# Low parts of the first tile's second half of keys, and of the gate sums, moved behind the second head's minimum in a planned attention and MLP kernel

## The chip, the cores and the metric

The kernel runs on one NeuronCore of a Trainium2 chip. The metric is device time in microseconds of one execution, as a median over timed runs. The core has five instruction queues that matter here: TensorE (PE in the profile, with its weight loads as PEld), VectorE (DVE), ScalarE (ACT), GpSimd (POOL) and SyncE (SP), which issues the DMA transfers.

## What is computed

Attention with a forget gate over 4 batches of 8 heads, 576 positions, head size 64, all in float32; then two MLPs, each over 2304 rows of 512:

```python
log_f = np.log(np.clip(f, 0.0001, 1.0))
cum = np.cumsum(log_f, axis=-1)
scores = q @ k.T / sqrt(64) + (cum[..., :, None] - cum[..., None, :])
attn = softmax(where(causal, -1e9, scores))
x = attn @ v                                  # heads side by side: 2304 x 512
h = x @ w_in                                  # d_ff 1024
solu = h * softmax(h)
x = (layernorm(solu) * g_ln) @ w_out
out = relu(x @ w2_in) ** 2 @ w2_out           # d_ff 2048
```

## The kernel before

**Split operands.** A float32 value is kept as a rounded high part and a low part, the difference, and a product is made of three products of parts. So each operand needs a copy or cast for its high part and a subtraction for its low part. For the scores, the two halves of TensorE's 128 rows carry the parts: `K1` holds high parts of the keys twice, `K2` holds the low parts in its first 64 rows and, below them, 16 rows with the parts of the gate sums (`cum`) of all heads; `Q2` has rows of zeros and ones there, its picks, that take the head's own row. `KN` and `QN` are the raw keys and queries as loaded. The index `j` is the half of the heads: `j = 0` for heads 0 to 3, `j = 1` for heads 4 to 7.

**Tiles and stages.** A tile is 128 (or, once a batch, 64) query positions of one batch, for all 8 heads; there are 20. `head(s)` puts down one head of one tile: the scores in a PSUM bank `z` (line 576, two matmuls a cut), the minimum over the masked row on VectorE (`least`, line 597), the exponential on ScalarE (line 611), transposes of the result by TensorE (line 630) and copies of them back to SBUF (line 376 on ScalarE, 382 on VectorE). `mix` multiplies with the values (line 650). Two banks `z` alternate between the heads, three buffers hold exponentials, three banks `pp` transposes. Where 128 rows of x are done, `first(x)` puts down the first MLP for them: matmuls (lines 869 to 871), a softmax and norm with two long ScalarE operations (887, 908), transposes of the result, and `out1` with the second half (lines 820 to 822). Between all this, the weights of the MLPs are split: line 729 and 378 on ScalarE, 733 and 737 on VectorE, 743 and 747 on GpSimd or VectorE. After about 450 us the second MLP runs.

**What sets the order.** Nothing is issued as it is written. `pl.add` makes a `Step` with a cost on each engine that may do it, a priority (a due time), and the keys that it reads and writes, from which its dependences follow. `Plan.lay` then walks a clock of its own: at each point it takes, on each engine, the ready step that can start first, and among those that can start within `slack` the one with the lowest priority. A step with several engines goes to the one that is free first. Steps marked `port=True` on VectorE and steps of GpSimd are laid one after the other in this clock. So a step that is moved changes what is ready when, and with it the choice of engine and the order of everything that follows.

In this clock, where TensorE would stand idle for over 400 ns in the first 140 us, `fill` puts in filler transposes (line 1706) that compute nothing, as many as fill 0.6 of the hole at 62 ns each.

**What the change touches.** At the start stand priorities of their own:

```python
SECOND, THIRD = 9900.0, 9000.0
```

`SECOND` is the due time of what the first tile's heads 4 to 7 need: the copies of keys and queries and their low parts (`prep_k`, low parts in line 498; `prep_q`, scalings in lines 378 to 384, low parts in line 541). `THIRD` is that of the gate sums beyond the first tile: the scan over 448 positions (named line 1575 in the profile), their high part (a copy on ScalarE, line 1606) and their low part (line 1609, `tensor_tensor` of 32 x 576). Both parts are written to DRAM (`cumd`, line 1554) and come back, spread over the heads, as the 16 rows of `K2` for each later tile (line 506). The first tile's heads start at due time 10000, later than both.

Of the kernel before, what the change touches and what calls it, by code (L numbers as in the profile page):

```python
# [27 lines left out]
class Plan:  # L28
# [11 lines left out]
        dve=dict(pe=230, dve=127, act=198, pool=203, dma=1230),  # L40
# [19 lines left out]
    def add(self, eng, fn, prio, reads=(), writes=(), take=None, uses=(), late=0, port=False, kind="r"):  # L60

        s = Step()
        s.eng, s.fn, s.prio, s.take, s.no, s.late = eng, fn, prio, take, len(self.steps), late
        deps = {}
        s.uses = tuple(uses) + ((take,) if take else ())
        for k in s.uses:  # L70
            self.users.setdefault(k, []).append(s)
        s.weak, s.port, s.kind = None, port, kind
        for k in reads:
            if k in self.writer:
                deps[self.writer[k].no] = self.writer[k]
            rs = self.readers.setdefault(k, [])
            if k in self.banks or k[0] in ("pp", "hp"):

                if rs and rs[-1].no not in deps:
                    s.weak = rs[-1]  # L80
                    deps[s.weak.no] = s.weak
            rs.append(s)
        for k in writes:
            if k in self.writer:
                deps[self.writer[k].no] = self.writer[k]
            for r in self.readers.get(k, ()):
                deps[r.no] = r
        for k in writes:
            self.writer[k] = s
            self.readers[k] = []  # L90
        deps.pop(s.no, None)
        s.deps = list(deps.values())
        s.succ = []
        for d in s.deps:
            d.succ.append(s)
        s.left = len(s.deps)
        s.rdy = {}
        s.end = None
        self.steps.append(s)
        return s  # L100

    def fill(self, order, ring, a, b, lag, share):
        ident = self.writer["ident"]
# [165 lines left out]
def tile_kernel(ctx: ExitStack, tc: tile.TileContext, q, k, v, f, w_in, w_out, g_ln, w2_in, w2_out, out):  # L269
# [23 lines left out]
    HH = H // 2  # L293
# [66 lines left out]
    pl = Plan(dict(pp=3, hp=2, rq=NRQ), ("z0", "z1", "xo", "h", "h0", "h1"))  # L360
# [83 lines left out]


    vslot = {}

    def load_k(n, prio):
        T = tiles[n]
# [36 lines left out]
    def prep_k(n, prio):  # L486
        T = tiles[n]
        m, b, q0 = T["m"], T["b"], T["q0"]
        kc = kcol(b, T["t"])
        cs = slice(kc, kc + m)  # L490
        los = {}
        for j in range(2):
# [15 lines left out]
            if n == 0 and j:  # L508
                prio = SECOND
# [6 lines left out]
                lo, prio + 2 * j, [("kn", j)] + hk, lk,  # L516
                port=True,
            )
            for y in range(2):
                rk = [f"cumd{y}"] if n else [("c0", 0), ("xh", 0, 0)][y : y + 1]  # L520
                pl.add(
                    dict(dma=350), lambda y=y, auxrows=auxrows: auxrows(y), (prio if n else -7e6) + 2 * j, rk,
                    writes=kcells(f"ka{y}", j, kc, kc + m),
                )

    def prep_q(n, prio):
        m = tiles[n]["m"]
        i = n % 2
        raw = QN[:, 0 : HH * m].rearrange("p (h s) -> p h s", s=m)
        for j, src in enumerate(own):  # L530
# [9 lines left out]
            def lo(src=src, q1=q1, hi=(q1 if j else q2)):  # L540
# [2 lines left out]
                    op1=ALU.subtract,  # L543
                )

            pl.add(
                dict(dve=67 + 1.045 * HH * m), lo, prio + 2 * j, ["qn", ("qd" if j else "qh", i, j)], [("ql", i, j)],
                port=True,
            )


    def head(s):
# [48 lines left out]

        for y, (c, k_) in enumerate(zip(cuts, zk)):
            w = c[2] - c[1]
            pl.add(
                dict(dve=77 + 1.042 * w + 61 * y), lambda y=y, c=c: least(y, c), prio,
                ["mask"] + [sk_ + (0,)] * y, [k_, sk_ + (y,)],
            )
# [962 lines left out]
    for y, (a, e) in enumerate(((0, P), (P, S))):  # L1570
# [33 lines left out]
        ["mhalf", ("lf", 0), ("lf", 1), ("qh", 0, 0), ("qd", 0, 0)], [("st", 0, 0)],  # L1604
    )
    pl.add(dict(act=573), lambda: nc.scalar.copy(part(0), cu), THIRD, ["cu0", "cu1"], pt0[0])
    pl.add(
        dict(dve=669),
        lambda: nc.vector.tensor_tensor(out=part(1), in0=cu, in1=part(0).bitcast(F32), op=ALU.subtract), THIRD,
        ["cu0", "cu1"] + pt0[0], pt0[1],  # L1610
# [38 lines left out]
    for n in range(NQ):  # L1649
        for h in range(H):  # L1650
# [7 lines left out]
            if h == PQ and n + 1 < NQ:  # L1658
                prep_q(n + 1, when[s])
                if n + 2 < NQ:  # L1660
                    load_q(n + 2, when[s])
            head(s)
            w = 4 if n >= QUADS else 2
            if (h + 1) % w == 0:
                mix(s, w)
# [129 lines left out]
```

## Time and profile before

| | us |
|---|---|
| median of 3 timed runs (lowest, highest) | 810.95 (810.48, 811.85) |
| the profiled execution, its own time | 813.03 |
| the profiled execution, its span | 811.2 |
| TensorE busy in the span | 790.8 (97%) |
| VectorE busy | 638.9 (79%) |
| ScalarE busy | 550.3 (68%) |
| GpSimd busy | 384.6 (47%) |

The span is what the hardware profiler saw between the first and the last instruction; the execution's own time has what lies around it as well. Busy times are sums over the span, and a share over the whole span mixes stages with different limits: the attention stage, up to some 450 us, keeps four engines going, while in the MLP stage behind it TensorE alone is at its limit. Fillers count as busy time of TensorE. The granted TensorE clock is 1.00 of full speed in every stretch up to 780 us.

### The profile page before, as it was taken

The page shows a single profiled execution, that of the slowest core. Times are in us where ns is not written, and L with a number is a line of the kernel's source. Part 1 is how long each engine was busy: PE and PEld are TensorE (multiplying, and loading weights), DVE is VectorE, ACT ScalarE, POOL GpSimd, SP SyncE. Part 2 cuts the span into 40 slices and gives each one's busy share as a digit, 9 for nine tenths or more (in the row PEclk, how much of TensorE's full clock was granted, in tenths as well). Part 3 has the DMA queues.
Part 4 walks back from the last instruction along what each step waited for, and adds up shares of the span by engine and source line. Part 5 has one row for each costly group of instructions (what it writes and reads, how often), then busy time and mean ns, then how long its engine had stood idle before and what let it go on. Part 6 is the DMA issues. An engine that isn't in the chain of part 4 may idle for free.

```text
span 811.2 us, 19134 instructions
## 1 busy us (share of the span) xinstructions
PE 790.8 (97%) x6607; PEld 726.7 (90%) x6607; DVE 638.9 (79%) x1627; ACT 550.3 (68%) x1425; POOL 384.6 (47%) x520
## 2 busy tenths in 40 slices
PE   7899999999999999999999999999999999999997
PEld 6677788888888888888989999999999999999997
DVE  8788788787786667886677879779778877987777
ACT  6899998889998888898886775445335343533442
POOL 6467778666778686777757622120211121112110
PEclk9999999999999999999999999999999999999999
DMA  6644346656664555665477899696767767675401
GB/s 216 206 117 140 105 128 186 206 173 190 199 206 163 189 171 165 196 229 180 169 247 232 265 309 368 213 321 212 229 207 233 230 203 223 216 232 186 159 1 53
DMA packets 109665, 159.69 MB, mean 197 GB/s; under 512 B 12832, under 2 KB 52768, under 8 KB 109568
## 3 DMA queue, kind: packets, MB, share of 16 engines
q1 hardware_dynamic: 109280, 158.21, 60.9%
q8 instruction: 52, 0.85, 0.4%
q14 instruction: 45, 0.37, 0.2%
q10 hardware_dynamic: 288, 0.26, 0.1%
HBM read 121.65 MB, written 36.72 MB: 195 GB/s over the span
## 4 chain that ended last, share of the span: by engine, by line
PE 47%; POOL 2%; DVE 2%; issue 1%; DMA 1%; ACT 1%; DVEq 0%; POOLq 0%
PE z L1392 9%; PE pp L1392 9%; PE hp L1497 4%; PE hp L1498 4%; PE hp L1499 4%; PE z L1341 3%; PE xo L1498 2%; PE xo L1499 2%; PE xo L1497 2%; DMA w2d<-free 1%; PE pp L1498 1%; PE pp L1499 1%; PE pp L1497 1%; PE pp L820 1%; PE pp L822 1%
## 5 line engine op out<-in xcount | busy, mean ns | idle before, releaser
L611 ACT ACTIVATE adj<-z,st 64x288 f32<-64x288 f32 (+9 forms) x192 | 95.0, 498 | 17.7 <-DVE st L597 15.9
L576 PE MATMUL z<-k,q 80*64 80x288 f32 (+17 forms) x384 | 89.9, 331 | 0.2
L597 DVE CUSTOM_DVE_ANT_0 z<-z,maskb 128x128 f32<-128x128 f32 (+8 forms) x144 | 65.3, 462 | 26.8 <-PE z L576 24.8
L630 PE MATMUL pp<-ident,adj 128*128 128x128 f32 (+1 forms) x480 | 76.4, 273 | 9.2 <-ACT adj L611 8.2
L821 PE MATMUL pp<-ln,wol 128*128 128x256 f32 x288 | 80.1, 278 | 0.0
L822 PE MATMUL pp<-ln,woh 128*128 128x256 f32 x288 | 80.1, 278 | 0.0
L630 PEld LDWEIGHTS pp<-ident,adj 128*128 128x128 f32 (+1 forms) x480 | 50.7, 140 | 32.4 <-ACT adj L611 22.4
L376 ACT COPY pt<-pp 128x384 f32<-128x384 f32 (+5 forms) x167 | 67.5, 422 | 15.2 <-PE pp L630 13.7
L1153 DVE TENSOR_TENSOR k<-adj,k 128x512 fp32r<-128x512 f32 (+1 forms) x71 | 48.9, 688 | 32.5 <-POOL k L380 25.2
L743 POOL TENSOR_TENSOR free<-free 128x256 uint32<-128x256 uint32 x64 | 49.1, 772 | 33.9 <-DVE free L737 20.7
L576 PEld LDWEIGHTS z<-k,q 128*128 128x128 f32 (+3 forms) x384 | 54.9, 176 | 8.3 <-ACT adj L611 4.1
L869 PE MATMUL hp<-wih,xl 128*128 128x512 f32 x144 | 60.0, 417 | 0.8 <-ACT hp L908 0.8
L650 PE MATMUL xo<-pt,vn 128*64 128x128 f32 (+1 forms) x960 | 60.4, 268 | 0.1
L650 PEld LDWEIGHTS xo<-pt,vn 128*64 128x64 f32 x960 | 48.6, 137 | 9.4 <-issue 5.4
L870 PE MATMUL hp<-wil,xh 128*128 128x512 f32 x144 | 56.6, 393 | 0.2 <-DVE wil L747 0.2
L871 PE MATMUL hp<-wih,xh 128*128 128x512 f32 x144 | 56.8, 394 | 0.0
L1106 POOL TENSOR_TENSOR free<-free 128x256 f32<-128x256 f32 x64 | 52.5, 821 | 7.5 <-DMA w2d<-free 4.8
L821 PEld LDWEIGHTS pp<-ln,wol 128*128 128x128 f32 x288 | 54.4, 189 | 0.4
L822 PEld LDWEIGHTS pp<-ln,woh 128*128 128x128 f32 x288 | 54.1, 188 | 0.0
L1098 POOL TENSOR_TENSOR free<-free 128x256 fp32r<-128x256 f32 x63 | 50.0, 805 | 7.4 <-ACT free L376 6.9
L380 POOL TENSOR_SCALAR k<-adj 128x512 fp32r<-128x512 f32 x37 | 23.1, 624 | 63.7 <-PE xo L1499 25.7
L1392 PE MATMUL z<-wol,k 128*128 128x256 f32 x384 | 52.4, 276 | 0.0
(614 smaller groups left out, 2682.4 us busy)
## 6 DMA issues: line engine op xcount, KB each, us to landing
k<-w2u SPq DMA_DIRECT2D x96, 256.0 KB
ln<-w2u SPq DMA_DIRECT2D x96, 256.0 KB
w2u<-free SPq DMA_DIRECT2D x56, 256.0 KB
kn<-in_k_dram SPq DMA_DIRECT2D x32, 256.0 KB
free<-in_moe_w_out_dram SPq DMA_DIRECT2D x32, 256.0 KB
free<-in_moe_w_in_dram SPq DMA_DIRECT2D x32, 256.0 KB
q<-w2u SPq DMA_DIRECT2D x32, 256.0 KB
w2f<-free SPq DMA_DIRECT2D x49, 128.0 KB
```

What stands on the lines that cost most here:

```text
L376: nc.scalar.copy(dst(), src())
L576: nc.tensor.matmul(dst, lhsT=ql[0:r, p, 0:m], rhs=rhs, start=(g == 0), stop=(g == 1))
L597: nc.vector.tensor_tensor_reduce(out=z, in0=z, in1=maskb[0:m, o : o + e - a], scale=1.0, scalar=st[0:m, 0:1] if y else 3e38, op0=ALU.add, ...
L611: nc.scalar.activation(out=adj[0:m, c[1] : c[2]], in_=Z[c[0]][0:m, 0 : c[2] - c[1]], func=AF.Exp, bias=st[0:m, low : low + 1], scale=-1.0, ...
L630: nc.tensor.transpose(at(sk)[:, (c - g) * m : (c - g + 1) * m], adj[0:m, zc : zc + P], ident[0:m, 0:m])
L650: nc.tensor.matmul(XO[own[j], g // 2, off : off + m], lhsT=VN[vslot[b, c]][:, (g + j) * D : (g + j + 1) * D], rhs=PT[(s - h + g + j) % NPT ...
L821: nc.tensor.matmul(px, lhsT=wol[:, fc, w], rhs=hi, start=False, stop=False)
L822: nc.tensor.matmul(px, lhsT=woh[:, fc, w], rhs=hi, start=False, stop=(fc == KF - 1))
L869: nc.tensor.matmul(HP[:, c], lhsT=XL[i][:, cc, :], rhs=wih[:, cc, w], start=(cc == 0), stop=False)
L871: nc.tensor.matmul(HP[:, c], lhsT=XH[i][:, cc, :], rhs=wih[:, cc, w], start=False, stop=(cc == KC - 1))
L1392: nc.tensor.matmul(half(i), lhsT=l, rhs=r[:, c * TB : c * TB + TB], start=(j == start), stop=(j == 5), skip_group_check=True,)
L1497: nc.tensor.matmul(po, lhsT=gl, rhs=wh, start=(p == 0 and i in opens), stop=False, skip_group_check=True)
```

## The change

It adds two dependences between steps of the plan and moves one priority by 2: no operation of the computation is added or removed. Two low parts may not start before the minimum of the first tile's head 1: that of the first tile's keys of heads 4 to 7, and that of the gate sums. (`least_of[1, 0]` is the step of that minimum; `held_back` gets one step, since only the first tile's `j = 1` is put in.) The low part of the first tile's queries of heads 4 to 7 gets the priority `SECOND` instead of `SECOND + 2`.

```diff
+    def after(self, s, d):
+        if d not in s.deps:
+            s.deps.append(d)
+            d.succ.append(s)
+            s.left += 1
...
+    held_back, least_of = [], {}
...
+            if n == 0 and j:
+                held_back.append(los[j])
...
-            pl.add(
-                dict(dve=67 + 1.045 * HH * m), lo, prio + 2 * j, ["qn", ("qd" if j else "qh", i, j)], [("ql", i, j)],
-                port=True,
+            s = pl.add(
+                dict(dve=67 + 1.045 * HH * m), lo, SECOND if n == 0 and j else prio + 2 * j,
+                ["qn", ("qd" if j else "qh", i, j)], [("ql", i, j)], port=True,
             )
...
-            pl.add(
+            least_of[s, y] = pl.add(
                 dict(dve=77 + 1.042 * w + 61 * y), lambda y=y, c=c: least(y, c), prio,
...
-    pl.add(
+    low_sums = pl.add(
         dict(dve=669),
...
             head(s)
+            if s == 1:
+                for x in held_back + [low_sums]:
+                    pl.after(x, least_of[1, 0])
```

The lines of the new file are 6 to 12 higher: 597 becomes 606, 498 becomes 505, 384 becomes 390, 541 becomes 550, 1609 becomes 1618, 482 becomes 489, 743 becomes 752, 747 becomes 756, 820 becomes 829, 576 becomes 585, 630 becomes 639, 947 becomes 956 and 1706 becomes 1718. What the plan makes of it is shown at three places.

VectorE, first tile, behind the scan of the gate sums. `k_8` is `K2` of heads 4 to 7, `q_20` is `Q2`, `q_42` is `Q1` of heads 4 to 7, `free` the gate sums, and the two rows that write `z` and `st` are minima (each with a row that reads the result out). Before:

```order
L498 TENSOR_TENSOR k_8_79<-kn_17_88,k_46_117 64x4x128
L384 TENSOR_SCALAR q_20_91<-qn_80 64x512
L1609 TENSOR_TENSOR free_92<-free_92 32x576
L597 ISA z_121,st_29_100<-z_121,maskb_71 128x128
L597 ISA st_29_100 128x1
L597 ISA z_122,st_30_101<-z_122,maskb_71 128x128
L597 ISA st_30_101 128x1
L384 TENSOR_SCALAR q_42_113<-qn_80 64x512
L541 SCALAR_TENSOR_TENSOR q_42_113<-qn_80,q_42_113 64x512
L597 ISA z_121,st_31_102<-z_121,maskb_71 128x128
```

Now:

```order
L390 TENSOR_SCALAR q_20_91<-qn_80 64x512
L390 TENSOR_SCALAR q_42_113<-qn_80 64x512
L550 SCALAR_TENSOR_TENSOR q_42_113<-qn_80,q_42_113 64x512
L606 ISA z_121,st_29_100<-z_121,maskb_71 128x128
L606 ISA st_29_100 128x1
L606 ISA z_122,st_30_101<-z_122,maskb_71 128x128
L606 ISA st_30_101 128x1
L1618 TENSOR_TENSOR free_92<-free_92 32x576
L505 TENSOR_TENSOR k_8_79<-kn_17_88,k_46_117 64x4x128
L606 ISA z_121,st_31_102<-z_121,maskb_71 128x128
```

The low part of the keys and that of the gate sums stood ahead of the first two minima and now stand behind them; the second scaling of the queries and their low part (now lines 390 and 550) stood behind and are now ahead.

GpSimd, from its picks (`q_20<-ident`) on. `k_7` and `k_8` in lines 498 and 505 are here the low parts of the second tile's keys, `ln` and `wil` parts of the first MLP's weights. Before:

```order
L482 TENSOR_TENSOR q_20_91<-ident_110 16x512
L380 TENSOR_SCALAR ln_50_209<-ln_50_209 128x512
L498 TENSOR_TENSOR k_7_78<-kn_16_87,k_45_116 64x4x128
L498 TENSOR_TENSOR k_8_79<-kn_17_88,k_46_117 64x4x128
L743 TENSOR_TENSOR ln_50_209<-ln_50_209 128x512
L380 TENSOR_SCALAR ln_50_209<-ln_50_209 128x512
L743 TENSOR_TENSOR ln_50_209<-ln_50_209 128x512
```

Now:

```order
L489 TENSOR_TENSOR q_20_91<-ident_110 16x512
L386 TENSOR_SCALAR ln_50_209<-ln_50_209 128x512
L752 TENSOR_TENSOR ln_50_209<-ln_50_209 128x512
L756 TENSOR_TENSOR wil_75<-ln_50_209,wih_74 128x512
L386 TENSOR_SCALAR q_20_91<-qn_80 64x512
L386 TENSOR_SCALAR ln_50_209<-ln_50_209 128x512
L752 TENSOR_TENSOR ln_50_209<-ln_50_209 128x512
```

The two low parts of the second tile's keys have left this queue. They are in VectorE's now: one ahead of the minimum of head 4 (the picks of line 489, which stood ahead of it, now behind it), one ahead of the minimum of head 7.

TensorE, in the first tile of 64 rows (the fifth tile), where each head has two cuts of 288 columns, up to the first matmuls of `out1`. Line 947 (now 956) transposes the normalised rows that `out1` needs. Before:

```order
L947 MATMUL pp_125<-ident_110,e_90 128x128 x4
L947 MATMUL pp_126<-ident_110,e_90 128x128 x4
L869 MATMUL hp<-wih_74,xl_38_109 128x512
L870 MATMUL hp<-wil_75,xh_37_108 128x512
L871 MATMUL hp<-wih_74,xh_37_108 128x512
L576 MATMUL z_121<-k_45_116,q_41_112 64x288
L576 MATMUL z_121<-k_7_78,q_20_91 64x288
L576 MATMUL z_122<-k_45_116,q_41_112 64x288
L576 MATMUL z_122<-k_7_78,q_20_91 64x288
L630 MATMUL pp_127<-ident_110,adj_28_99 128x64 x5
L820 MATMUL pp_125<-ln1a_857,woh_76 128x256
```

Now:

```order
L585 MATMUL z_122<-k_45_116,q_41_112 64x288
L585 MATMUL z_122<-k_7_78,q_20_91 64x288
L639 MATMUL pp_127<-ident_110,adj_27_98 128x64 x5
L1718 MATMUL pp_126<-ident_110 128x128 x18
L956 MATMUL pp_126<-ident_110,e_90 128x128 x4
L956 MATMUL pp_125<-ident_110,e_90 128x128 x4
L585 MATMUL z_121<-k_46_117,q_42_113 64x288
L585 MATMUL z_121<-k_8_79,q_20_91 64x288
L1718 MATMUL pp_127<-ident_110 128x128 x10
L585 MATMUL z_122<-k_46_117,q_42_113 64x288
L585 MATMUL z_122<-k_8_79,q_20_91 64x288
L829 MATMUL pp_127<-ln1a_817,woh_76 128x256
```

The transposes and the first matmul of `out1` stood ahead of and right behind the third head of this tile; they now stand behind the fourth and the fifth, and fillers stand around them. In the whole program there are 227 fillers, where there were 215; up to the start of this tile 189, where there were 208. The steps that ScalarE, VectorE and GpSimd share are dealt out anew as well: ScalarE has 1192 operations instead of 1201, GpSimd 538 instead of 525, VectorE 1607 instead of 1611, each counted with repeats. The last 2479 matmuls of TensorE, of 6129 before, are in the same order in both.

## Rows read from the trace of the kernel before

**Rows 1.** Page: the span, and TensorE's busy time, share and instructions.

```profile
span 811.2 us, 19134 instructions
...
PE 790.8 (97%) x6607; PEld 726.7 (90%) x6607; DVE 638.9 (79%) x1627; ACT 550.3 (68%) x1425; POOL 384.6 (47%) x520
```

**Rows 2.** Busy time by stretch (start:end, length, each engine, clock, DMA share, GB/s).

```profile
8.00:32.00 24.00, 17.76 (x137) 13.97 (x135) 19.68 (x46) 17.42 (x51) 11.86 (x10) 1.00 0.72 222
32.00:60.00 28.00, 27.14 (x209) 21.57 (x205) 24.09 (x54) 27.06 (x69) 15.46 (x14) 1.00 0.52 154
60.00:100.00 40.00, 38.54 (x282) 30.11 (x284) 31.81 (x79) 38.59 (x98) 30.05 (x46) 1.00 0.42 128
...
500.00:811.20 311.20, 306.57 (x2686) 306.16 (x2684) 247.04 (x657) 124.53 (x256) 48.71 (x83) 1.00 0.61 199
```

**Rows 3.** The same by stretch for line 1706 (fillers) alone.

```profile
8.00:32.00 24.00, 8.82 (x69) 7.34 (x67) 1.00 0.72 222
32.00:60.00 28.00, 8.02 (x62) 7.00 (x62) 1.00 0.52 154
60.00:100.00 40.00, 5.19 (x44) 4.82 (x44) 1.00 0.42 128
```

**Rows 4.** Timeline, VectorE, 5 to 12 us (start, us, engine, line, operation, operands).

```profile
5.33 0.67 DVE L498 TENSOR_TENSOR k<-kn,k 64x512 fp32r<-64x512 f32 x1
...
7.94 1.45 DVE L498 TENSOR_TENSOR k<-kn,k 64x512 fp32r<-64x512 f32 x1
9.41 0.42 DVE L384 TENSOR_SCALAR q<-qn 64x512 fp32r<-64x512 f32 x1
9.86 0.75 DVE L1609 TENSOR_TENSOR free<-free 32x576 fp32r<-32x576 f32 x1
10.54 0.28 DVE L597 CUSTOM_DVE_ANT_0 z<-z,maskb 128x128 f32<-128x128 f32 x1
...
11.62 0.69 DVE L541 SCALAR_TENSOR_TENSOR q<-qn,q 64x512 fp32r<-64x512 f32 x1
```

**Rows 5.** Timeline, GpSimd, 7 to 30 us.

```profile
7.16 1.69 POOL L482 TENSOR_TENSOR q<-ident 16x512 fp32r<-16x512 f32 x1
...
13.57 3.03 POOL L498 TENSOR_TENSOR k<-kn,k 64x512 fp32r<-64x512 f32 x2 [0.52 <-ACT k L376]
...
28.78 1.30 POOL L743 TENSOR_TENSOR ln1a<-ln1a 128x512 uint32<-128x512 uint32 x1 [1.46 <-ACT k L376]
```

**Rows 6.** Timeline, ScalarE: exponentials of heads 0, 4, 7 and the second tile's first.

```profile
10.91 0.37 ACT L611 ACTIVATE adj<-z,st 128x128 f32<-128x128 f32 x1 [2.19 <-DVE st L597]
...
17.62 0.37 ACT L611 ACTIVATE adj<-z,st 128x128 f32<-128x128 f32 x1 [2.40 <-DVE st L597]
...
23.08 0.37 ACT L611 ACTIVATE adj<-z,st 128x128 f32<-128x128 f32 x1
...
27.23 0.47 ACT L611 ACTIVATE adj<-z,st 128x256 f32<-128x256 f32 x1
```

**Rows 7.** Timeline, VectorE, 13 to 18 us: picks, and minima of heads 4 and 5.

```profile
13.56 0.69 DVE L737 SCALAR_TENSOR_TENSOR ln<-ln 128x512 uint32<-128x512 uint32 x1
14.28 2.87 DVE L482 TENSOR_TENSOR q<-ident 16x512 fp32r<-16x512 f32 x1
17.18 0.30 DVE L597 CUSTOM_DVE_ANT_0 z<-z,maskb 128x128 f32<-128x128 f32 x1
...
17.50 0.29 DVE L597 CUSTOM_DVE_ANT_0 z<-z,maskb 128x128 f32<-128x128 f32 x1
```

**Rows 8.** TensorE: group of fillers, 8 to 100 us; timeline, first matmul of line 820.

```profile
L1706 PE MATMUL pp<-ident 128*128 128x128 f32 x175 | 22.2, 274 | 0.0
...
98.20 0.39 PE L820 MATMUL pp<-ln1a,woh 128*128 128x256 f32 x1
```

**Rows 9.** Groups by form, ScalarE, 20 to 130 us: scaling of weights.

```profile
L378 ACT ACTIVATE xc<-xc,gcol 128x256 f32<-128x256 f32 x7 | 3.6, 509 | 0.4 <-POOL xc L743 0.2
```


## The prediction, on record before the changed kernel ran

> **What bounds the kernel now.** I read the page's totals first: TensorE is busy 790.8 of 811.2 us [rows 1]. That hides two kinds of lost time, so the second view is the table by stage [rows 2] beside the same table for line 1706 alone, the filler transposes that compute nothing [rows 3]. From 500 us on TensorE works 306.57 of 311.20 us and nothing ahead of it can be seen to matter except when that stage begins. From 8 to 32 us it is busy 17.76 of 24 us, and 8.82 of that is filler; between 32 and 100 us it is busy 65.68 of 68 us, with 13.21 of filler. So up to 100 us about 8.6 us of idling (6.24 + 0.86 + 1.46) and 22 us of filler are time in which TensorE had no real work. ScalarE is busy 65.65 of 68 us between 32 and 100 us [rows 2]: there it is the engine that the others wait for, while from 8 to 32 us it idles 6.58 us. A gain must therefore come out of the first 32 us, must be handed on by ScalarE's full queue up to 100 us, and then moves the whole TensorE-bound rest.
>
> Where the first 32 us go is in the timelines. VectorE finishes the scan at 7.94 us, and then the low part of the keys of heads 4 to 7 takes 1.45 us [rows 4] where the same operation took 0.67 us a little earlier. Beside it GpSimd ran its picks from 7.16 to 8.85 us [rows 5], and VectorE ended 0.54 us after them. Only then follow one scaling of q (0.42 us), the low gate sums (0.75 us) and, at 10.54 us, the first head's minimum. ScalarE, idle for 2.19 us, starts the first exponential at 10.91 us [rows 6]. The second hole is larger: VectorE's picks take 2.87 us, from 14.28 us [rows 7], because GpSimd computes two low parts of the second tile's keys from 13.57 to 16.60 us [rows 5]; VectorE again ends 0.55 us after it. So head 4's minimum starts at 17.18 us, its exponential at 17.62 us after 2.40 us of idling [rows 6], and head 7's exponential comes only at 23.08 us, the second tile's first at 27.23 us.
>
> **The change, heads 0 to 3.** Ahead of the first minimum, 0.67 + 0.75 = 1.42 us go away and a scaling (0.42) and a low part of q (0.69) come in, 1.11 us: 0.31 us are gained, no more. The wait for GpSimd's picks stays: it now falls on the scaling of q. The page on SBUF in the Trainium skill ("SBUF — State Buffer", Who interferes with whom) says that the port pair which VectorE and GpSimd share is an exclusive lock, and that VectorE's tensor_scalar in its two-port mode takes it. By that the scaling waits until 8.85 us as the low part did, which is what the sum has; without a lock it would end at 7.94 + 0.42 us, and the first exponential would gain 0.78 us more (1.45 - 0.67). The trace agrees with the lock for the low part (1.45 against 0.67 us); it has no such scaling beside GpSimd in the first 10 us.
>
> Between the second and the third minimum lay 1.11 us (scaling, low part of q); now it is the two moved operations, 1.42 us. Starting 0.31 us earlier they end about where the old pair did, so heads 2 and 3 gain 0.2 us. The moved steps delay two transfers behind them: the write of the gate sums' low part, and the next load of the keys of heads 4 to 7, whose buffer the low part reads. Both slip about 1 us; what reads them is the second tile's scores, over 10 us later, so I cost them at nothing. If that cover were gone they would cost that 1 us.
>
> **Heads 4 to 7.** Here is most of the gain, and it is a consequence, not the stated move: the plan is laid anew, and both low parts of the second tile's keys leave GpSimd's queue for VectorE's. Head 4's minimum now comes behind one of them and ahead of the picks. VectorE's operation of line 737 ends at 14.25 us (13.56 + 0.69 [rows 7]); a low part is 0.67 us if GpSimd is not in the way, 1.45 if it is [rows 4]. I take 0.67, because GpSimd's next operation needs the very result that ends at 14.25, while the low part already stands in VectorE's queue. Head 4's minimum then starts at 14.9 instead of 17.18, its exponential at 15.3 instead of 17.62: 2.3 us. The picks now meet GpSimd's addition, 1.30 us where it ran alone [rows 5]; started behind the low part it ends at 16.2, the picks 0.55 us later, and head 5's minimum starts at 16.75 instead of 17.50. From there ScalarE's own row of work decides: from 16.2 us two casts, two scalings, three short copies and two exponentials, some 3.8 us by the spacing in its timeline, put head 7's exponential at 20.1 instead of 23.08 us, 3.0 us earlier. Up to the second tile's first exponential ScalarE now has eight operations (4.1 us) and about 1.1 us of waits for the sums and the transposes of x, where it had five. That makes 25.3 instead of 27.23 us: **a gain of 1.9 us** handed to the full stage. Its bounds are 0.3 us (nothing beyond heads 0 and 1 stays) and 3.0 us (what head 7 gains).
>
> **The stage behind it.** Two things can be counted in the new order. ScalarE loses work: over the program 1192 operations instead of 1201, and five of the nine are gone ahead of the 41st exponential. A typical one is 0.51 us [rows 9], so 2.55 us leave an engine that is 97% busy there. Between nothing and 2.55 us I take half, **1.3 us**, since TensorE is as full as ScalarE and GpSimd, which takes the work, also holds up VectorE. On the other side the plan has 227 fillers instead of 215. A filler is 22.2/175 = 0.127 us [rows 8], so twelve are 1.5 us. They stand where the plan sees holes, and only some will stand in the way: between nothing and 1.5 us I take half, **0.8 us lost**.
>
> Sum: -1.9 - 1.3 + 0.8 = -2.4 us. The profiled execution has a span of 811.2 us and took 813.03 us; the median of the three timed runs is 810.95 us, so the span is taken as the measure of change, and 2.4 us off the median give **808.6 us**. A measurement of this kernel tells about 0.2%, 1.6 us, from no change, so faster means under 809.3 us and slower over 812.6 us.
>
> **Rivals.** First, that the gain is lost in the full stage: the start is 0.3 to 1.9 us earlier, the new order hands back as much, and the time stays at 811 us. For it speaks that ScalarE and TensorE are both full from 32 to 100 us and that the order changes on every engine up to about 400 us, with gains and losses that no row of before can show; against it, that a start which is earlier on ScalarE, TensorE and VectorE alike has nothing to wait for except transfers.
>
> Second, slower: a hole at the first tile of 64 rows. In the old order the matmuls of line 820 (the first MLP's second half) follow the scores of that tile's third head, at 98.20 us [rows 8], and no filler stands in that tile: from there TensorE has always something to do. In the new order they come behind the fifth head's scores, and 38 fillers stand in the tile ahead of them, 10 + 18 + 10. If the normalised rows that they need are not ready earlier than before, 38 x 0.127 = 4.8 us of filler is real waiting; less the 1.9 us gained at the start, the run ends 2.9 us later, at 813.8 us. The point that decides is whether the first matmul of that line (829 in the new file) starts before or after 98.2 us, with two more heads done. For it speaks that fillers are set where the plan sees a hole of over 400 ns; against it, that the new order has fewer fillers up to that tile (189 against 208) and that the ScalarE work ahead of it is no more than before.
>
> Third, that the change doesn't do what it says: the order shows that the low parts do stand behind the second minimum, so only the plan's further moves are open; the time would be the 0.31 us of heads 0 and 1, and it goes with the first rival.
>
> **Chances.** The forecast has 0.50, with a range of its own from 806 to 809.3 us (the far end: 3.0 + 2.55 us off, with no filler in the way, is 805.4). The first and third rival together have 0.24, the hole 0.26. The range from 806.0 to 814.0 takes in the forecast, the unchanged time and the hole at its price, and leaves out the far ends on both sides, under 2 in 10.
>
> **What the new profile would show.** The first exponential at 10.6 us, head 4's minimum near 14.9 and head 7's exponential near 20.1 us would bear out the first part; the second tile's first exponential near 25.3 us its sum. Idle time of ScalarE from 8 to 32 us should fall from 6.58 us to some 4.5. If head 4's minimum still lies beyond 16.5 us, GpSimd's addition has got ahead of the low part and the gain at the start is under 1 us. If the first matmul of line 829 lies beyond 98.2 us, the second rival has it. And if the start is earlier by 2 us but the 200 us mark shows TensorE with no more work done than before, the full stage has eaten it.

## The result: 0.56% slower, and the profile after

The changed kernel takes 815.54 us (median of 6 runs, 815.06 to 817.98) against 811.65 us before (6 runs, 810.48 to 811.91): ratio 1.0056, 95% interval 1.0042 to 1.0070 (4.5 us by the ratio, 3.9 by the two medians). The forecast was 808.6 us, in a range from 806.0 to 814.0: the sign and the range are both wrong. The page of the profile after, which answers to [rows 1], has 2.2 us more of TensorE in a span 2.4 us longer:

```profile
span 813.6 us, 19154 instructions
...
PE 793.0 (97%) x6619; PEld 728.9 (90%) x6619; DVE 640.7 (79%) x1623; ACT 549.3 (68%) x1416; POOL 391.8 (48%) x533
```

**The start came much as forecast.** VectorE after, first tile (columns as in [rows 4]). The two scalings behind the scan take 1.84 us together: in the trace's single records the first takes 0.66 us and the second 1.17, and they end 0.28 and 0.29 us behind one operation of GpSimd each (its cast of keys, 6.60 + 1.39, and its picks, 8.07 + 1.09). The low part ahead of head 4's minimum takes 0.68 us, as the forecast chose between 0.67 and 1.45.

```profile
6.44 1.13 DVE L1584 TENSOR_TENSOR_SCAN free<-e,free 32x448 f32<-32x448 f32 x1
7.60 1.84 DVE L390 TENSOR_SCALAR q<-qn 64x512 fp32r<-64x512 f32 x2
...
13.93 0.68 DVE L505 TENSOR_TENSOR k<-kn,k 64x512 fp32r<-64x512 f32 x1
14.54 0.28 DVE L606 CUSTOM_DVE_ANT_0 z<-z,maskb 128x128 f32<-128x128 f32 x1
...
14.91 1.40 DVE L489 TENSOR_TENSOR q<-ident 16x512 fp32r<-16x512 f32 x1
...
16.98 1.32 DVE L505 TENSOR_TENSOR k<-kn,k 64x512 fp32r<-64x512 f32 x1
```

GpSimd after, beside the scan and the scalings:

```profile
6.60 1.39 POOL L386 TENSOR_SCALAR k<-kn 128x512 fp32r<-128x512 f32 x1 [1.68 <-DMA kn<-in_k_dram]
8.07 1.09 POOL L489 TENSOR_TENSOR q<-ident 16x512 fp32r<-16x512 f32 x1
```

And the scan of before, which took longer:

```profile
6.53 1.49 DVE L1575 TENSOR_TENSOR_SCAN free<-e,free 32x448 f32<-32x448 f32 x1
```

ScalarE's exponentials of heads 0, 4, 7 and the second tile's first, after, to set beside [rows 6]:

```profile
10.59 0.37 ACT L620 ACTIVATE adj<-z,st 128x128 f32<-128x128 f32 x1 [2.32 <-DVE st L606]
...
14.97 0.37 ACT L620 ACTIVATE adj<-z,st 128x128 f32<-128x128 f32 x1
...
19.86 0.37 ACT L620 ACTIVATE adj<-z,st 128x128 f32<-128x128 f32 x1
...
25.45 0.47 ACT L620 ACTIVATE adj<-z,st 128x256 f32<-128x256 f32 x1
```

They lead [rows 6] by 0.32, 2.65, 3.22 and 1.78 us. The forecast had 10.6, 15.3, 20.1 and 25.3 us.

**What took it back.** Busy time by stretch of after (columns as in [rows 2]; the granted clock is the third number from the end):

```profile
8.00:32.00 24.00, 20.16 (x143) 16.02 (x141) 21.48 (x48) 18.30 (x54) 13.30 (x12) 0.93 0.74 227
14.00:18.00 4.00, 3.92 (x21) 3.36 (x21) 3.92 (x10) 3.50 (x12) 3.02 (x3) 0.57 0.88 281
32.00:60.00 28.00, 26.95 (x218) 21.64 (x216) 25.16 (x58) 26.84 (x66) 17.40 (x17) 1.00 0.56 167
60.00:100.00 40.00, 38.29 (x294) 31.04 (x293) 33.89 (x80) 37.61 (x103) 27.03 (x41) 1.00 0.36 112
100.00:200.00 100.00, 97.63 (x798) 83.40 (x797) 79.03 (x213) 86.03 (x249) 75.39 (x97) 1.00 0.57 174
200.00:300.00 100.00, 97.51 (x777) 84.53 (x776) 73.68 (x197) 86.39 (x245) 77.73 (x103) 1.00 0.57 181
300.00:400.00 100.00, 97.82 (x844) 83.12 (x843) 70.08 (x197) 88.19 (x256) 73.99 (x99) 1.00 0.60 192
400.00:500.00 100.00, 99.84 (x818) 94.58 (x818) 81.54 (x162) 72.86 (x180) 54.52 (x71) 1.00 0.80 265
```

The fillers alone (line 1718) in three of these stretches, beside [rows 3]:

```profile
8.00:32.00 24.00, 9.14 (x66) 7.91 (x64) 0.93 0.74 227
32.00:60.00 28.00, 8.95 (x68) 7.83 (x68) 1.00 0.56 167
60.00:100.00 40.00, 6.66 (x55) 6.08 (x56) 1.00 0.36 112
```

And the stretches of before that [rows 2] does not show:

```profile
14.00:18.00 4.00, 2.21 (x14) 1.47 (x14) 3.77 (x6) 1.58 (x8) 4.00 (x3) 1.00 0.89 298
...
100.00:200.00 100.00, 98.21 (x818) 83.49 (x815) 81.49 (x221) 89.71 (x266) 70.02 (x90) 1.00 0.57 175
200.00:300.00 100.00, 99.15 (x803) 86.32 (x803) 75.10 (x202) 89.47 (x252) 78.37 (x105) 1.00 0.57 179
300.00:400.00 100.00, 98.67 (x836) 84.56 (x833) 75.73 (x207) 84.28 (x250) 73.33 (x99) 1.00 0.61 198
400.00:500.00 100.00, 98.65 (x825) 94.32 (x824) 77.81 (x158) 74.14 (x183) 50.74 (x61) 1.00 0.82 267
```

Busy time does not add up to work here: part of it is fillers, and at the lower clock a matmul is busy for longer. So count columns: a matmul of 128x256 has 256, and by the rows of the two traces both kernels have 1,537,024 without their fillers. After is 3,584 columns ahead at 32 us; up to 141 us that is used up (192 behind at 100, 640 ahead at 141), and then it falls to 768 behind at 200, 5,472 at 300 and 7,424 at 400 us. Before does 1,796 columns in a us from 100 to 400 us, so the last figure is worth 4.1 us, near what the medians and the ratio say. (The two spans differ by 2.4 us only, because the profiled execution of before was 1.4 us above its median.) So nearly the whole loss is made between 141 and 400 us, most of it from 200 to 300. The exponentials say the same: the 41st still leads before's by 2.55 us, the 65th by 0.39, and the 129th is 4.93 us late.

Three places stand out. The clock in 14 to 18 us is at its lower level, 1.2 GHz, for most of the stretch (0.57). Ahead of it TensorE of after waited 0.67, 0.51 and 0.35 us between 10.4 and 14.1 us, and the nine fillers that before has at 12.88 and 15.63 us are not there. The hole of the second rival is there; TensorE of after in that tile:

```profile
93.62 1.31 PE L1718 MATMUL pp<-ident 128*128 128x128 f32 x10
...
96.72 2.19 PE L1718 MATMUL pp<-ident 128*128 128x128 f32 x18
98.75 1.04 PE L956 MATMUL pp<-ident,e 128*128 128x128 f32 x8
99.54 0.51 PE L585 MATMUL z<-k,q 128*64 128x288 f32 x2
99.89 1.26 PE L1718 MATMUL pp<-ident 128*128 128x128 f32 x10
100.99 0.48 PE L585 MATMUL z<-k,q 128*64 128x288 f32 x2
101.30 0.28 PE L829 MATMUL pp<-ln1a,woh 128*128 128x256 f32 x1
```

Line 829 starts at 101.30 us, 3.1 us behind [rows 8]. And from 141 to 400 us TensorE waits more. The two groups that hold most of its idle time there (the transposes of the exponentials and of x; last comes the idle time before them and what ended it), before:

```profile
L630 PE MATMUL pp<-ident,adj 128*128 128x128 f32 (+1 forms) x306 | 48.3, 274 | 2.7 <-ACT adj L611 2.3 <-DVE ln1a L950 0.3
...
L676 PE MATMUL pp<-ident,x 128*128 128x128 f32 (+1 forms) x52 | 7.7, 270 | 0.4 <-ACT x L376 0.4
```

and after:

```profile
L639 PE MATMUL pp<-ident,adj 128*128 128x128 f32 (+1 forms) x303 | 48.2, 275 | 4.3 <-ACT adj L620 3.8
...
L685 PE MATMUL pp<-ident,x 128*128 128x128 f32 (+1 forms) x52 | 7.8, 273 | 2.3 <-ACT x L382 1.8 <-DVE ln1a L959 0.5
```

6.6 us against 3.1, nearly all of it waiting for results of ScalarE, in waits of 0.2 to 1.0 us.

### The profile page after: what moved, and what is told of

Same layout as the page of the kernel before. It is cut to its first block, busy times and chain, and to the rows that moved or that the text cites. A ratio compares the mean times of both kernels' runs of the same rounds, so it can differ in the third digit from the quotient of the medians.

```text
span 813.6 us, 19154 instructions
## 1 busy us (share of the span) xinstructions
PE 793.0 (97%) x6619; PEld 728.9 (90%) x6619; DVE 640.7 (79%) x1623; ACT 549.3 (68%) x1416; POOL 391.8 (48%) x533
## 4 chain that ended last, share of the span: by engine, by line
PE 52%; ACT 3%; DVE 2%; issue 1%; DVEq 0%; ACTq 0%
PE pp L1401 9%; PE z L1401 9%; PE hp L1507 4%; PE hp L1508 4%; PE hp L1506 4%; PE z L1350 3%; PE xo L1507 2%; PE xo L1508 2%; PE xo L1506 2%; PE pp L829 1%; PE pp L831 1%; PE pp L830 1%; PE xo L659 1%; PE pp L1507 1%; PE pp L1508 1%; PE pp L1506 1%
## 5 line engine op out<-in xcount | busy, mean ns | idle before, releaser
L585 PE MATMUL z<-k,q 128*128 128x256 f32 (+17 forms) x384 | 89.1, 331 | 0.2 <-DVE q L550 0.2
L382 ACT COPY pt<-pp 128x256 f32<-128x256 f32 (+5 forms) x167 | 66.8, 419 | 16.4 <-PE pp L639 14.8
L752 POOL TENSOR_TENSOR free<-free 128x256 uint32<-128x256 uint32 x64 | 52.2, 820 | 35.7 <-DVE free L746 21.4
```

The lines of the kernel that those rows point to most:

```text
L382: nc.scalar.copy(dst(), src())
L585: nc.tensor.matmul(dst, lhsT=ql[0:r, p, 0:m], rhs=rhs, start=(g == 0), stop=(g == 1))
```

## The experiments

In most of them the plan is laid twice in one program, with the edit (`news`) and without it (`olds`). The edits are printed shortened: names such as `scaling`, `between`, `gap` and `start` (the fillers of the new start with fillers, below) stand for lines that pick out these steps. `spliced(until(a, x), b)` follows the list `a` up to step `x` and then `b`, leaving out what is done. "The k-th exponential leads by" compares its start in two traces.

### Stated moves alone, and new start or new rest alone

```diff
-    order = pl.lay(SLACK)
+    order = olds
+    for x in held:
+        order = moved(order, x, least_of[1, 0], 1)
+    for x in (scaling, low_q):
+        order = moved(order, x, least_of[0, 0], 0)
```

> The order of before on every engine; only VectorE's first tile is rearranged by hand to the changed kernel's row (scaling and low part of q ahead of the first minimum, the two low parts behind the second). Theory A (the stated moves cost nothing themselves; what the plan does anew is the loss): first exponential near 10.6 us, time within 0.8 us of before. Theory B (the moves delay the gate sums or the key buffer): 813 us or more.

Measured: ratio 0.9999 (0.9987 to 1.0010).

```diff
+    order = spliced(until(news, scores_of[12]), olds)
```

> The order of the changed kernel up to the scores of the second tile's head 4 (about 34 us), then the order of before, step by step, with its engines. Theory A (the start gains 2 us, the loss comes from the new order of everything behind it): faster than before by about 2 us, 809 to 811 us. Theory B (the start itself costs, by its queues or its slower TensorE clock between 14 and 18 us): as before or slower, 811.5 to 815.5 us. Both expect the second tile's first exponential near 25.5 us.

Measured: ratio 1.0000 (0.9989 to 1.0010).

```diff
+    order = spliced(until(olds, scores_of[12]), news)
```

> The counterpart: the order of before up to the scores of the second tile's head 4, then the changed order. Theory A: slower than the changed kernel, or like it where the lead is lost anyway, 815.5 to 818 us. Theory B: near the time before, 811 to 813 us.

Measured: ratio 1.0065 (1.0053 to 1.0077), 5.3 us. So the loss sits in what the plan lays behind 34 us, and the start neither causes nor pays for it. But by the leads in their traces the first two should have been faster. With the moves alone the second tile's third exponential led before by 1.29 us and its fourth came 0.35 us late. TensorE there waited, and then thirteen fillers took 2.98 us:

```profile
25.01 1.11 PE L690 MATMUL pp<-ident,x 128*128 128x128 f32 x4 [1.13 <-ACT x L383]
...
27.47 2.98 PE L1723 MATMUL pp<-ident 128*128 128x128 f32 x13
```

The stretch of that run shows why: from 24 to 32 us the granted clock is 0.57.

```profile
24.00:32.00 8.00, 6.99 (x35) 6.56 (x37) 5.20 (x16) 5.64 (x16) 3.24 (x4) 0.57 0.55 191
```

A caution on leads of a single trace: most of those 1.29 us come from VectorE's picks, which took 1.64 us there and 2.87 in before. In the last of these three runs, the old start, whose first tile has before's order, they took 1.65 us too, and its second tile starts at 25.92 instead of 27.23 us, without any moved step. Two more traces with that order have 2.88 and 2.89 us. So this part of a lead can come and go with the order unchanged.

### Fillers that keep the clock up

The fillers are more of the same transposes, put where TensorE idled.

```diff
+    order = filled(order, {turn_of[0]: 2, mix_of[3]: 3, turn_of[7]: 8, scores_of[8]: 4, spread_of[0]: 9})
```

> The order of before with only VectorE's first tile rearranged, as in the run of the moves alone, and 26 filler matmuls more where TensorE idled there (2, 3, 8, 4 and 9 of them, ahead of the first head's transpose, of the second pair's products, of the eighth head's transpose, of the second tile's first scores and of the first tile's result transposes). In that run the second tile's first three exponentials led before by 1.3 us, then the granted clock stood at 0.5 from 24 to 32 us, thirteen fillers took 2.98 us in place of 1.58, and the fourth exponential came 0.35 us later than in before. Theory A (the fall of the clock eats the lead): the clock stays at 0.97 or above to 36 us, the fourth exponential of the second tile starts near 32.0 and the time falls by 1.3 us, ratio 0.998. Theory B (the full stage behind would have taken the lead anyway): the clock stays up and the lead at the fourth exponential may be there, but the ratio is 0.9995 to 1.001. Rival C (more fillers delay the work): ratio above 1.001.

Measured: ratio 0.9992 (0.9983 to 1.0001). The clock is 1.00 from 8 to 36 us and the thirteen fillers take 1.59 us, as theory A has it; but the fourth exponential starts at 32.53, not 32.0, and what is left is 0.6 us, half of what was expected and within what can be told from nothing.

```diff
+    order = spliced(until(news, scores_of[12]), olds)
+    order = filled(order, {turn_of[0]: 6, turn_of[2]: 4, turn_of[3]: 3, turn_of[8]: 4, turn_of[9]: 2, turn_of[10]: 9})
```

> The changed order up to the scores of the second tile's fifth head, then that of before, as in the run of the changed start, and 28 fillers more where TensorE idled there (6, 4 and 3 in the first tile, 4, 2 and 9 in the second). There the clock stood at 0.5 from 14 to 20 us and near 0.5 to 0.7 from 30 to 34, the exponentials led before by 2.2 us in the middle of the second tile, by 1.64 at its fourth head and by 0.15 to 0.2 from the third tile on. Theory A (the fall of the clock eats the lead): the clock stays up, the lead at the third tile is 1.2 to 2.0 us, ratio 0.9975 to 0.9985. Theory B (the full stage takes the lead anyway): ratio 0.9995 to 1.001.

Measured: ratio 0.9979 (0.9970 to 0.9988). Theory A: the lead at the third tile is 1.71 us where the same order without the fillers had 0.15, and it lasts (1.39 us still at 346 us). Some 0.2 us of it is this execution's earlier scan (6.20 us, against 6.44). This version beats both kernels. Its stretch beside the one above:

```profile
24.00:32.00 8.00, 7.69 (x56) 6.19 (x55) 7.96 (x16) 6.66 (x19) 4.03 (x4) 1.00 0.60 186
```

```diff
+    order = filled(olds, {turn_of[0]: 6, turn_of[4]: 8, turn_of[7]: 4, spread_of[0]: 9, turn_of[8]: 5})
```

> The kernel before with 32 fillers more in the idle stretches of its first two tiles (6, 8, 4, 9 and 5, ahead of transposes that TensorE waited 1.22, 1.84, 0.55, 1.14 and 0.65 us for), nothing moved. Theory A (the gain of the changed start with fillers comes from the moved steps, the fillers only keep the clock): before's clock is 1.00 already, ratio 0.9990 to 1.0010. Rival B (the fillers alone win): ratio 0.997 to 0.9985.

Measured: ratio 0.9995 (0.9986 to 1.0004). The fillers alone win nothing.

```diff
+    order = filled(news, {turn_of[0]: 5, turn_of[2]: 4, turn_of[3]: 3})
```

> The changed kernel with 12 fillers more in the first tile (5, 4 and 3), where nine of before's are missing and the clock fell to 0.57 from 14 to 18 us. Theory A (the loss of the change comes from its order behind the start, 34 to 400 us): the clock stays up, the first tile ends up to 0.3 us earlier, the ratio to before stays at 1.004 to 1.007. Rival B (the loss is that fall of the clock): ratio at or below 1.002.

Measured: ratio 1.0056 (1.0041 to 1.0072), the change's own. The clock stayed at 1.00 from 14 to 18 us and fell to 0.57 from 30 to 34 instead, so it was put off rather than cured, and this run alone does not free the clock of the loss. A run further below does, with the changed order from 141 us on alone: it loses without any low clock.

### The hole in the first 64-row tile

```diff
+    order = [y for y in news if not (is_fill(y) and between(y, scores_of[32], out_of[0]))]
```

> The changed kernel without the 38 fillers in the first tile of 64 rows, GpSimd's order as it is. If the fillers themselves stand in the way (4.8 us of them, of which the last 28 come ahead of the awaited matmul): 812.5 to 814.5 us. If they only fill a wait for the normalisation: 815 to 816 us.

Measured: ratio 1.0102 (1.0086 to 1.0119). Without its 38 fillers the kernel is slower by 0.0046 of 811.6, 3.7 us. The first output matmul starts at 100.86, only 0.44 us earlier. Stretches of this run:

```profile
92.00:100.00 8.00, 5.05 (x49) 3.47 (x48) 6.33 (x16) 7.90 (x25) 5.79 (x8) 0.96 0.37 118
100.00:106.00 6.00, 5.69 (x27) 5.33 (x28) 4.33 (x12) 4.33 (x13) 3.97 (x7) 0.50 0.34 92
```

and of after:

```profile
92.00:100.00 8.00, 7.99 (x79) 6.63 (x78) 6.61 (x14) 7.44 (x25) 5.67 (x8) 1.00 0.37 115
100.00:106.00 6.00, 6.00 (x66) 5.53 (x65) 5.42 (x12) 5.23 (x15) 3.96 (x7) 1.00 0.30 90
```

TensorE idles 3 of 8 us and then gets 27 matmuls done where after does 66, ten of them fillers.

```diff
+    order = moved(news, norm_of[1], scale_and_shift, 1)
+    order = [y for y in order if not (is_fill(y) and between(y, scores_of[32], out_of[0]))]
```

> The changed kernel with GpSimd's normalisation of the second 128 rows (line 939, at 96.84 us) put right behind the operation that it waits for (line 933, at 84.13 us), and without the 38 fillers in the first tile of 64 rows. If that late normalisation makes the hole (theory A1): first matmul of the first MLP's second half near 98 us, 812 to 814 us. If not: 815 to 816 us.

Measured: ratio 1.0093 (1.0077 to 1.0108). The normalisation ended 12.8 us earlier (85.33 instead of 98.16) and the transposes came at 96.28, yet the first output matmul again waited to 100.86: the scores ahead of it waited 1.51 and 0.96 us for exponentials, behind weight operations on ScalarE. GpSimd's late normalisation by itself is not what binds.

```diff
+    order = moved(news, norm_of[1], scale_and_shift, 1)
+    gap[1].fill = 8
+    order = [y for y in order if y is not gap[2]]
+    order = moved(order, exp_of[35, 0], least_of[35, 1], 1)
+    order = moved(order, exp_of[35, 1], exp_of[35, 0], 1)
...
```

> The changed kernel with the hole in the first 64-row tile put in order by hand: the normalisation of the second 128 rows right behind its scale and shift on GpSimd, that tile's fourth head's two exponentials and the copies of the normalised rows ahead of the weight operations on ScalarE, the transposes of these rows ahead of the hole's fillers on TensorE, and of the 28 fillers there 8 left. Theory A (the hole comes from the order on three engines together, and not from the fillers): the first matmul of the output weights starts at 98.5 to 99.5 in place of 101.30, the clock stays up, and the time falls by 2 us to 813.5, ratio 1.002 to 1.004. Rival B (fewer fillers let the clock fall, as in the two runs without them): clock at 0.5 behind 98 us and ratio 1.007 to 1.010. Rival C (the full stage behind absorbs it): first matmul early, ratio as the change's, 1.0045 to 1.0065.

Measured: ratio 1.0098 (1.0079 to 1.0116); none of the three as written. The kernel came into the tile 1.9 us later than the change did, with a low clock at 14 to 20 and 30 to 34 us. From the fourth head's scores to the first output matmul it took 4.1 us where after takes 5.7, so the hole was shortened by 1.6 us. But 5 us later TensorE waited twice for ScalarE. The copy that ends the first wait stood behind a weight scaling, for which ScalarE had itself waited 1.99 us for GpSimd:

```profile
106.63 0.80 PE L666 MATMUL xo<-pt,vn 128*64 128x64 f32 x18 [1.10 <-ACT pt L383]
108.52 0.48 PE L590 MATMUL z<-k,q 128*64 128x288 f32 x2 [1.08 <-ACT adj L626]
```

From 109.4 to 112 us the granted clock was 0.50. The wait was moved, not removed.

### Where in the new order

```diff
+    order = spliced(until(news, out_of[0]), olds)
```

> The changed order up to the first matmul of the first MLP's second half (101.3 us in the changed kernel, 98.2 before), then the order of before. By the non-filler work of TensorE up to 100 us (60.65 us against 61.41) the changed kernel is 0.8 us behind there. If the hole in the first tile of 64 rows has already cost the loss (theory A1): 814 to 815.5 us. If the loss comes mostly after 100 us (theory A2): 811.5 to 813 us.

Measured: ratio 1.0070 (1.0055 to 1.0085): 816.5 us, above both ranges.

```diff
+    order = spliced(until(olds, out_of[0]), news)
```

> The order of before up to the same matmul, then the changed order. Theory A1: 811.5 to 813 us. Theory A2: 814 to 816 us.

Measured: ratio 1.0148 (1.0133 to 1.0162): neither theory. The clock is 0.5 from 102 to 108 us, right behind the seam, and much of this is the seam's own price. The next three therefore carry the fillers of the good start and differ from it in one stretch.

```diff
+    order = filled(spliced(until(news, scores_of[24]), olds), start)
```

> The run of the new start with fillers, but with the changed order kept to the scores of the fourth tile's first head (62 us) and before's from there. At that point the changed order has laid 28 steps more than before's at the same scores. Theory A (the loss lies in the hole of the first 64-row tile and behind): ratio as that run's, 0.9965 to 0.9990, the hole's first output matmul at 96 to 97.5 us. Rival B (the loss is made ahead of it, because the new order spends the lead on those 28 steps and lays the rest too thin): ratio 1.001 or above.

Measured: ratio 1.0005 (0.9997 to 1.0014), 2.1 us worse than with the seam at 34 us. The first output matmul came at 98.21.

```diff
+    order = filled(spliced(until(news, scores_of[32]), olds), start)
```

> The same with the changed order kept to the scores of the fifth tile's first head (88 us, where the 64-row tiles begin), before's order behind it. Theory A (the loss lies in the hole): ratio 0.9965 to 0.9995. Rival B (the hole is the price of what was laid ahead of it, since the weight work done early leaves the tile with other work beside it): ratio 1.003 to 1.007, as in the run with the changed order to the first output matmul (1.0070).

Measured: ratio 1.0034 (1.0023 to 1.0045). Here too a seam has its part: TensorE waits 3.84 us at 86.6 us for a copy of x on ScalarE, and the clock falls to 0.5 at 92.

```diff
+    order = filled(spliced(until(spliced(until(news, scores_of[12]), olds), scores_of[64]), news), start)
```

> The run of the new start with fillers, and the changed order again from the scores of the ninth tile's first head (141 us) to the end. Theory A (the later stage of the new order costs 2 us in small waits of its own): ratio 1.0000 to 1.0020, that is 2 to 3 us above that run, with more idle time of TensorE between 141 and 400 us. Rival B (the small waits of the whole change come from the hole's delay, not from the later order): ratio 0.9970 to 0.9990.

Measured: ratio 1.0025 (1.0015 to 1.0035), so the order behind 141 us alone costs 0.0046 against the new start with fillers (0.9979), 3.7 us, more than expected. There is no low clock up to 400 us, and its waits from 141 to 400 us are like the change's own, 7.6 us in these groups against 2.9 in the run that it differs from (2.5 and 0.4):

```profile
L645 PE MATMUL pp<-ident,adj 128*128 128x128 f32 (+1 forms) x301 | 47.4, 274 | 5.5 <-ACT adj L626 5.3
...
L692 PE MATMUL pp<-ident,x 128*128 128x128 f32 (+1 forms) x48 | 7.2, 272 | 2.1 <-ACT x L383 1.7 <-DVE ln1a L967 0.4
```

What is late in these waits is mostly not ScalarE's own work. Of these waits, taking those over 0.15 us, 5.7 of 7.4 us end at an exponential or a copy of x ahead of which ScalarE had stood idle 0.3 to 1.2 us for a minimum or the sums from VectorE; in the run that it differs from that is 1.5 of 2.6 us, in the change 4.4 of 6.1, in before 1.5 of 3.0. One of 0.97 us, the same in this run and in the change, shows how. In the change's trace TensorE has six matmuls laid between a head's scores and its transposes (367.62 to 368.49 us), but minimum and exponential take until 369.31:

```profile
367.32 0.46 PE L585 MATMUL z<-k,q 128*128 128x320 f32 x2
...
368.13 0.50 DVE L606 CUSTOM_DVE_ANT_0 z<-z,maskb 128x320 f32<-128x320 f32 x1
...
368.78 0.53 ACT L620 ACTIVATE adj<-z,st 128x320 f32<-128x320 f32 x1 [1.15 <-DVE st L606]
...
369.45 0.55 PE L639 MATMUL pp<-ident,adj 128*128 128x128 f32 x3 [0.97 <-ACT adj L620]
```

The longest wait of this run, 1.60 us at 161.31 us, the change does not have, so the seam at 141 us may have a part in the 3.7 us. From 200 us on ten of its eleven waits stand in the change's trace too, within 0.1 us in length.

### Half of the edit

The plan is laid with one of the two steps held back, and the priority left as before. (`held` has the low part of the keys first, then that of the gate sums.)

```diff
-    order = pl.lay(SLACK)
+    order = laid(True, held[:1], False)
```

> Before, planned anew with the low part of the keys held back and that of the gate sums not. The plan differs on every engine from both kernels. Theory A (chance of the new plan): anywhere from 809 to 818 us, and ordered like TensorE's non-filler work up to 120 us. Theory C (the held keys are what costs): 814.5 to 816.5 us, like the changed kernel.

Measured: ratio 1.0144 (1.0126 to 1.0162), with the first output matmul at 106.31, 8.1 us behind before's.

```diff
-    order = pl.lay(SLACK)
+    order = laid(True, held[1:], False)
```

> The plan laid anew with only the low part of the gate sums held back behind the second head's minimum. Theory A (any new laying falls somewhere within a spread of 1 per cent, whatever piece was held): no value is forecast beyond 0.998 to 1.015, and the lead at the fourth tile's scores says nothing about the end. Rival B (the held low part of the keys makes the loss): ratio 1.000 within 0.001, with the order behind the first tile as before's.

Measured: ratio 1.0055 (1.0039 to 1.0070). Its first output matmul came at 96.92, ahead of before's 98.20, so this kernel has no hole and still loses as much as the change. Its 33rd exponential leads by 1.74 us, its 161st is 7.74 us late.

## Why the prediction was wrong, point by point

- **Heads 0 to 7: the times right, not all of their parts.** Starts and durations held within 0.45 us, but for head 2, which gained 0.76 us and not 0.2; ScalarE's idle time from 8 to 32 us fell to 5.70 us, not to 4.5. The 0.31 us ahead of the first minimum are partly luck: the scalings took 1.84 us where the sum had 0.42 each and a wait of 0.78, and the scan took 1.13 instead of 1.49 us, which the sum did not have. Where the scan took 1.49 us as in before (the change with twelve fillers more), 0.2 us were gained from the scan's start to the first minimum. That the scaling waits for GpSimd's picks came out: it ends 0.28 us behind their end (8.07 + 1.09). That agrees with the lock of the Trainium skill's page "SBUF — State Buffer" (Who interferes with whom).
- **"A gain of 1.9 us handed to the full stage": right in size, but on a condition that was not in the sum.** With before's order behind it the new start is worth 1.7 us (0.9979) when fillers keep TensorE at 2.4 GHz and nothing (1.0000) when they do not; the fillers alone gave 0.9995, within the noise. I read the clock of before as a constant; it hangs on the idle stretches and fillers that the plan was about to change.
- **"The stage behind it", -1.3 + 0.8 us: the step that failed, in sign.** I priced the new order there by what it has fewer or more of, nine ScalarE operations less and twelve fillers more, and not by what TensorE would wait for in it. On before's start the order behind 34 us costs 5.3 us (1.0065, with a seam and a granted clock of 0.85 from 20 to 30 us in it), and from 141 us on alone it costs 3.7 us (1.0025 against 0.9979), by exponentials and copies of x that TensorE waits for. Fewer operations did not help, since ScalarE itself stood idle ahead of most of these.
- **Twelve fillers, +0.8 us, within that step:** I priced a filler at 0.127 us, as if the wait were made of fillers. What the twelve cost was not measured; but in the hole fillers stand in a wait that is there anyway, and without 38 of them the kernel is 3.7 us slower.
- **Second rival (the hole, 0.26): its decider fell on its side, its mechanism does not carry the result.** The hole is there, 3.1 us late; but at 100 us TensorE is only 192 columns behind, no edit of the hole won anything, and the kernel with the sums alone held has none and is as slow.
- **First rival (the full stage eats the gain):** nearest to what happened, and its sign at 200 us came true (768 columns behind), but it stopped at no change. It did not reckon that a new laying can cost more than the start brings. Three layings of this plan with an edit of one or two steps gave 1.0056, 1.0144 and 1.0055, though the same steps moved by hand gave 0.9999.

What stays open. Against the new start with fillers the change has lost 6.2 us by the ratios (4.5 lost and 1.7 not kept). By columns it is 1,024 behind that run at 141 us and 11,392 at 400 us, 0.6 and 6.3 us at 1,796 in a us, so most is lost behind 141 us; the late order alone gave 3.7 of it, and where the rest comes from is not shown. The seams at 62 and 88 us cost 2.1 and 4.5 us against the seam at 34, but have waits of their own, and the prices do not add. Nor is shown why the planner's later order is poorer as a whole; only where TensorE waits in it, and at one of these waits, that too little was laid to cover the way from scores to transposes.

## What to carry to other kernels

When an edit goes through a planner, price the order it lays everywhere, not the place of the edit: move the same steps by hand in the old order first, and splice the new start onto the old rest, as here, where that, with fillers, was worth 0.2% and the whole laying cost 0.56%. Before counting an earlier start as a gain, look at the granted clock of the stretch behind it in the new profile. Fillers standing in a wait are not its cost; take them away and the matmuls behind may pay.

## What the runs showed of the hardware that was not expected

A wait of TensorE can be paid twice. With the moves alone it waited 1.02 and 1.13 us ahead of 22.3 and 25.0 us, then ran at the lower level (0.57 granted from 24 to 32 us), and thirteen fillers took 2.98 instead of 1.59 us. Behind the hole without fillers the granted clock was 0.50 from 100 to 106 us: a matmul of 256 columns took 0.41 us instead of 0.28, and starts lay 0.21 us apart instead of 0.12. By the Trainium skill's page "TensorE: Matmul & The Clock Gate" (Part 1) a gate lowers that clock to 1.2 GHz when the array idles; the two levels in these rows agree. But before waited 1.84 us ahead of 18.13 us and kept 1.00, so one wait's length does not tell.
